# Attention and MoE kernel: which late weight parts a transfer adds, and where the second products stand at the two changes of block

## The chip, the cores and the metric

The kernel runs on one core of a Trainium2 chip. The metric is the device time of one execution in microseconds (us), median of several runs. Engines are named as the profile names them: PE (TensorE matmuls), PEld (its weight loads), DVE (VectorE), ACT (ScalarE), POOL (GpSimd), SP (SyncE, which here only issues DMAs).

## The reference

Linear attention feeds a two-layer MLP. All data are float32.

```python
q_s = softmax(q, over head_dim); k_s = softmax(k, over seq)   # 8 batches, 8 heads, 576 x 64
kv  = einsum('bhsd,bhse->bhde', k_s, v)
x   = einsum('bhsd,bhde->bhse', q_s, kv)      # reshaped to 4608 tokens x 512
h   = x @ w_in                                # 512 x 2048
out = (h * clip(h + 3, 0, 6) / 6) @ w_out     # 2048 x 512
```

The weights come as float64 and are turned into float32 on the chip.

## The kernel before

**Blocks and chunks.** The 4608 tokens are nine blocks j of 512. The 2048 hidden columns are 16 chunks f of 128; a chunk is one slice of w_in (512 x 128) and one of w_out (128 x 512). Every float32 operand of a product is kept as two parts, `hi` (rounded to float32r) and `lo` (what is left of it), and each product is three matmuls: hi by hi, hi by lo, lo by hi. `split` (L121) makes them: ACT casts hi, DVE subtracts lo.

**Weights.** `decode(f)` (L136) makes chunk f's parts. Its steps are ACT L148, DVE L149, L151 and L155, ACT L158, DVE L159 (the value `v` is complete), ACT L167 or L123 (hi). Then for f below 10 DVE subtracts lo; for f from 10 to 15 ACT writes lo = -v (L168) and a DMA from POOL's queue adds to it (L169). `hi` and `lo` there cover both halves of the chunk: `parts[:, 0]` is w_in's (`wi[f]`), `parts[:, 1]` is w_out's (`wo[f]`). The tile `v` has three buffers under one tag, and x's copies, the transposed q and `fast_weights`' sums take turns in the same three.

**Blocks 0 and 1.** `gemm1(j, f)` (L562) is the first product of a chunk: 12 matmuls `ph`, of which the third is the first one to read lo of w_in. ACT L572 and DVE L573 make g, `split` makes g_hi and g_lo. `gemm2` (L579) is the second product: 12 matmuls `po`, in block 0 from chunk 0 to 15, into four PSUM banks that stay open over all 16 chunks. The list `pend` holds second products that are not issued yet; `fill_one` (L674) issues the oldest whole, `fill(n)` (L665) issues n matmuls. In block 0 one second product stays back behind the newest; in block 1 none does (`1 - j`, L696). From block 1 on PE's instructions keep the order in which they are written (`in_order`, L684); in block 0 a scheduler orders them. `store` (L596) empties the four banks through the tile `ob` (two buffers), by turns on ACT and DVE.

**Attention** for the next block runs beside this as steps of a generator (`steps`, L636). A block's x comes out of `px` (four head pairs). For block 1, ACT and DVE cut px into x_hi and x_lo, and gemm1 of block 1 reads them. From block 2 on `x_factors` (L424) makes seven sums of x.

**Blocks 2 to 8** do the first products of a pair of chunks in seven products of half size (`fast_pair`, L498: `pz` and `ph`, 6 matmuls of 256 columns each) instead of eight. For that `fast_weights(pair)` (L451) makes sums of w_in's four quarters: two DVE adds L459 build the whole values, DVE L466, L467, L469 and L470 make four sums in two `ob` tiles, `split` writes their parts over the pair's own `wi` tiles, and SP stores them to DRAM (L456, L473). `fetch` (L486) loads the seven factors back into the tiles of chunks 6 to 11 as a ring. For pairs 0 to 6 `fast_weights` runs in block 1; for pair 7 it runs in the first pair of block 2, after the fourth `slot`. `slot(n)` (L703) issues n matmuls of the second products and, on its second and fourth call, one step of attention. Within `fast_pair`, ACT L524, L530, L534 and DVE L527, L535, L554 take the products out of PSUM; the results of a pair go into the tiles of chunks 12 to 15 (`places`, L520).

Of the kernel before, what the change touches and what calls it, by code (L numbers as in the profile page):

```python
# [10 lines left out]
F32 = mybir.dt.float32  # L11
# [3 lines left out]
ALU = mybir.AluOpType  # L15
# [15 lines left out]
def attention_moe(  # L31
# [27 lines left out]
    nc = tc.nc  # L59
# [5 lines left out]
    NFC = w.shape[0]  # L65
# [45 lines left out]
    def place(f, dt, name):  # L111
        return wp.tile([P, 4 * DM], dt, name=name, tag=f"w{f}")
# [6 lines left out]
    wi, wo, raws = {}, {}, {}  # L119

    def split(hi, lo, src, engine=nc.vector):  # L121

        nc.scalar.copy(hi, src)  # L123
        engine.tensor_sub(lo, src, hi.bitcast(F32))  # L124
# [9 lines left out]
    BY_DMA = 10  # L134

    def decode(f):  # L136

        n = 2 * DM
        pairs = raws.pop(f).rearrange("p (n two) -> p n two", two=2)
        low, high = pairs[:, :, 0], pairs[:, :, 1]
        v = moe.tile([P, n], F32, name="v", bufs=3)
        m = v
        nc.scalar.activation(m, high.bitcast(F32), AF.Abs)  # L148
        nc.vector.tensor_scalar(m, m, W_MIN, W_MAX, op0=ALU.max, op1=ALU.min)  # L149
        m = m.bitcast(U32)  # L150
        nc.vector.tensor_scalar(  # L151
            m, m, 3, 0x3FFFFFFF, op0=ALU.logical_shift_left, op1=ALU.bitwise_and
        )
        vu = v.bitcast(U32)
        nc.vector.scalar_tensor_tensor(  # L155
            vu, high, 0xC0000000, m, op0=ALU.bitwise_and, op1=ALU.bitwise_or
        )
        nc.scalar.activation(low, low, AF.Copy, scale=2.0**-29)  # L158
        nc.vector.tensor_tensor(vu, vu, low, op=ALU.add)  # L159
        parts = place(f, F32R, f"w_{f}").rearrange("p (s i n) -> p s i n", s=2, i=2)  # L160
        vs = v.rearrange("p (s n) -> p s n", s=2)
        if f < 10:
            split(parts[:, :, 0], parts[:, :, 1], vs)
        else:

            hi, lo = parts[:, :, 0], parts[:, :, 1]
            nc.scalar.copy(hi, vs)  # L167
            nc.scalar.mul(lo, vs, -1.0)  # L168
            nc.gpsimd.dma_start(lo.bitcast(F32), vs, accum_op=ALU.add)  # L169
        wi[f], wo[f] = parts[:, 0], parts[:, 1]  # L170

    FAST = 2
# [277 lines left out]

    def fast_weights(pair):  # L451

        a, b = wi[2 * pair], wi[2 * pair + 1]
        kept[pair] = d = dr.tile([P, 7, 2, HT], F32, name=f"wf{pair}")
        for n, src in ((A11, a[:, :, 0:HT]), (A12, a[:, :, HT:]), (A22, b[:, :, HT:])):
            nc.sync.dma_start(d[:, n], src.bitcast(F32))  # L456
        whole = moe.tile([P, 2 * DM], F32, name="m", tag="v", bufs=3)
        for at, src in ((0, a), (TB, b)):
            nc.vector.tensor_add(  # L459
                whole[:, at : at + TB], src[:, 0].bitcast(F32), src[:, 1].bitcast(F32)  # L460
            )
        a11, a12, a21, a22 = (whole[:, n * HT : (n + 1) * HT] for n in range(4))
        hi, lo = (t.rearrange("p e n -> p (e n)") for t in (a, b))
        s12, s34 = (moe.tile([P, DM], F32, name="ob", bufs=2) for _ in range(2))
        s1, s2, s3, s4 = (t[:, n : n + HT] for t in (s12, s34) for n in (0, HT))
        nc.vector.tensor_add(s1, a21, a22)  # L466
        nc.vector.tensor_sub(s2, s1, a11)  # L467
        split(hi[:, 0:TB], lo[:, 0:TB], s12)
        nc.vector.tensor_sub(s3, a11, a21)  # L469
        nc.vector.tensor_sub(s4, a12, s2)  # L470
        split(hi[:, TB:], lo[:, TB:], s34)
        for e, t in enumerate((hi, lo)):
            nc.sync.dma_start(  # L473
                d[:, S1 : S4 + 1, e], t.bitcast(F32).rearrange("p (k n) -> p k n", k=4)
            )
# [22 lines left out]
    def fast_pair(j, pair, fill):  # L498

        to = factors(j)  # L500
        x = ps_h.tile([P, TB], F32, name="ph", tag="ph")[:, 0:HT]
        y = ps_h.tile([P, TB], F32, name="ph", tag="ph")[:, 0:HT]
        z = ps_a.tile([P, TB], F32, name="pz", tag="pa")[:, 0:HT]
        seen = set()

        def product(n, ps, name):
            w_hi, w_lo = (come[j, pair, n][:, e] for e in (0, 1))
            f_hi, f_lo = (to[ORDER[n][1]][:, e] for e in (0, 1))
            for i in range(2):
                c = slice(i * P, (i + 1) * P)  # L510
                for k, (w, f) in enumerate(((w_hi, f_hi), (w_hi, f_lo), (w_lo, f_hi))):
                    first = name not in seen
                    seen.add(name)
                    mm(ps, w[:, c], f[:, i], first, i == 1 and k == 2, True)
            del come[j, pair, n]
            fetch(1)

        first = moe.tile([P, TB], F32, name="first", tag="g_hi", bufs=3)
        second = moe.tile([P, TB], F32, name="second", tag="g_lo", bufs=3)
        places = [wi[12 + 2 * (pair % 2) + n] for n in (0, 1)]  # L520
        product(0, z, "z")
        product(1, x, "x")
        with tc.high_priority():
            nc.scalar.copy(first[:, 0:HT], x)  # L524
        fill(4)
        product(2, y, "y")
        nc.vector.tensor_add(first[:, 0:HT], first[:, 0:HT], z)  # L527
        product(3, x, "x")
        with tc.high_priority():
            nc.scalar.copy(second[:, 0:HT], x)  # L530
        fill(7)
        product(4, x, "x")
        with tc.high_priority():
            nc.scalar.copy(second[:, HT:], x)  # L534
            nc.vector.tensor_add(second[:, HT:], second[:, HT:], y)  # L535
        fill(7)
        product(5, x, "x")
        r = moe.tile([P, TB], F32, name="g", bufs=2)
        with tc.high_priority():
            nc.scalar.activation(r[:, HT:], x, AF.Relu, bias=three, scale=1.0)  # L540
            nc.vector.scalar_tensor_tensor(  # L541
                r[:, HT:], r[:, HT:], 6.0, x, op0=ALU.min, op1=ALU.mult
            )
        h = first[:, 0:HT]
        nc.scalar.activation(r[:, 0:HT], h, AF.Relu, bias=three, scale=1.0)
        nc.vector.scalar_tensor_tensor(
            r[:, 0:HT], r[:, 0:HT], 6.0, h, op0=ALU.min, op1=ALU.mult
        )
        gs = [(places[0][:, 0], places[0][:, 1])]
        split(*gs[0], r)  # L550
        fill(6)
        product(6, y, "y")
        with tc.high_priority():
            nc.vector.tensor_add(second[:, 0:HT], second[:, 0:HT], y)  # L554
        r = moe.tile([P, TB], F32, name="g", bufs=2)
        nc.scalar.activation(r, second, AF.Relu, bias=three, scale=1.0)  # L556
        nc.vector.scalar_tensor_tensor(r, r, 6.0, second, op0=ALU.min, op1=ALU.mult)  # L557
        gs.append((places[1][:, 0], places[1][:, 1]))
        split(*gs[1], r)
        return gs  # L560
# [89 lines left out]
    pend = []  # L650
# [14 lines left out]
    def fill(n=10**6):  # L665
        while pend and n:
            got = next(pend[0], None)
            if got is None:
                pend.pop(0)
                continue  # L670
            got[0](*got[1])
            n -= 1

    def fill_one():  # L674
        for fn, x in pend.pop(0):
            fn(*x)

    for j in range(FAST):
        for f in range(NFC):
            if j == 0:  # L680
                if f + AHEAD < NFC:
                    load_w(f + AHEAD)
            elif not in_order:
                in_order.append(True)  # L684
            g = gemm1(j, f)
            if j == 0:
                if f + 2 < NFC:
                    decode(f + 2)
            elif f % 2:
                if f < 15:  # L690
                    fast_weights(f // 2)
                if f >= 7:
                    fetch(1 if f < 15 else 12 - len(come))
            next(step, None)

            while len(pend) > 1 - j:  # L696
                fill_one()
            pend.append(work(j, [f], [g]))
    for j in range(FAST, NB):
        for pair in range(NFC // 2):  # L700
            done = [0]

            def slot(n):  # L703
                fill(n)
                done[0] += 1
                if done[0] in (2, 4):
                    next(step, None)
                if j == FAST and not pair and done[0] == 4:
                    fast_weights(NFC // 2 - 1)

            gs = fast_pair(j, pair, slot)
            fill()
            pend.append(work(j, [2 * pair, 2 * pair + 1], gs))
# [60 lines left out]
```

## Time and profile before

| what | value |
|---|---|
| median of 3 runs | 892.21 us (889.02 to 894.39) |
| profiled execution, its own time | 890.79 us |
| its span, first to last instruction | 888.9 us |
| PE busy, share of the span | 858.4 us, 97% |
| DVE / ACT / POOL busy | 614.6 / 464.8 / 132.9 us |
| mean granted TensorE clock | 0.99 |
| block 0 ends, block 1 begins (PE) | about 144 us |
| block 1 ends, block 2 begins (PE) | about 244 us |

The time of an execution is 1.9 us more than its span. PE is the engine that ends the chain; what counts is therefore when PE waits, and at which clock it runs. In the timeline a row has the start in us, the busy time, the engine, the line, the operation with its tiles, and in brackets the idle time ahead of it and what ended that. In the windows a row has the stretch, its length, then the busy time of PE, PEld, DVE, ACT and POOL, the granted clock, the DMA share and GB/s. Most helpers record under one line (L91 is every matmul, L123 every cast of a split, L124 every subtraction of one), so tiles tell more than lines.

### The profile page before, as it was taken

Reading aid. Unit: us, or ns where it says so; the run is one execution under the profiler, and the core shown is the slowest. Engines: PE = TensorE matmul, PEld = TensorE weight load, DVE = VectorE, ACT = ScalarE, POOL = GpSimd, SP = SyncE. Lnnn points to the kernel's source line nnn. Section 1 sums busy time; section 2 is a strip of 40 time slices with the busy share of each in tenths; the row PEclk is TensorE's granted clock in tenths of the full one; section 3 lists DMA queues with packets and bytes.
Section 4 is the critical chain, followed back from the end, with each engine's and each line's share of the span. In section 5 each row is a group of like instructions: output and inputs, shape, how many; then the busy total and the mean of one; then the engine's idle time right before and its main releaser. Section 6 shows DMA issues by size and latency. Waiting matters only on the chain.

```text
span 888.9 us, 15262 instructions
## 1 busy us (share of the span) xinstructions
PE 858.4 (97%) x5380; PEld 739.2 (83%) x5380; DVE 614.6 (69%) x1266; ACT 464.8 (52%) x944; POOL 132.9 (15%) x329
## 2 busy tenths in 40 slices
PE   5799998999999999999999999999999999999998
PEld 3578776787789888888888888888888888889896
DVE  7999867899777766767585757676867565444333
ACT  7998753544445454545454545444554554434333
POOL 5000132021212110202020202021212120100000
PEclk9899999999999999999999999999999999999999
DMA  9992583538487668676777668676755575567541
GB/s 372 413 369 84 125 203 136 180 108 289 161 259 224 219 202 258 216 224 203 228 233 229 209 220 259 200 230 195 256 158 183 161 230 170 167 178 224 170 140 47
DMA packets 98474, 185.19 MB, mean 208 GB/s; under 512 B 9824, under 2 KB 24160, under 8 KB 96352
## 3 DMA queue, kind: packets, MB, share of 16 engines
q1 hardware_dynamic: 96192, 180.03, 62.3%
q0 software_dynamic: 1632, 3.15, 2.0%
q10 hardware_dynamic: 576, 1.05, 0.3%
q8 instruction: 43, 0.70, 0.3%
q14 instruction: 31, 0.25, 0.1%
HBM read 156.93 MB, written 24.12 MB: 204 GB/s over the span
## 4 chain that ended last, share of the span: by engine, by line
PE 83%; DVE 7%; DMA 6%; ACT 2%; issue 1%; POOL 0%; SPq 0%; ACTq 0%; DVEq 0%; POOLq 0%
PE po L91 41%; PE ph L91 33%; PE pz L91 4%; PE px L91 2%; PE pkv L91 2%; DMA w<-v 2%; DMA qt<-in_qf_dram 2%; DVE w L124 1%; DMA out_dram<-ob 1%; DVE v L155 1%; DVE v L149 0%; DMA wf<-w 0%; POOL swap L289 0%; DVE km L267 0%; DVE v L159 0%
## 5 line engine op out<-in xcount | busy, mean ns | idle before, releaser
L91 PE MATMUL po<-w,w 128*128 128x512 f32 x1008 | 260.8, 394 | 0.8 <-ACT w L123 0.8
L91 PEld LDWEIGHTS po<-w,w 128*128 128x128 f32 x1008 | 178.4, 189 | 30.7 <-ACT w L123 1.1
L91 PE MATMUL ph<-x_lo,w 128*128 128x256 f32 (+1 forms) x800 | 152.2, 305 | 2.7 <-DVE x_lo L124 2.3
L91 PEld LDWEIGHTS ph<-w,w 128*128 128x128 f32 x1008 | 133.8, 190 | 11.0 <-DVE second L535 1.4
L91 PE MATMUL ph<-x_hi,w 128*128 128x256 f32 (+1 forms) x592 | 138.4, 338 | 4.4 <-DMA w<-v 3.3
L91 PE MATMUL ph<-w,w 128*128 128x256 f32 x1008 | 140.4, 284 | 1.2 <-DVE second L535 1.2
L91 PEld LDWEIGHTS ph<-x_lo,w 128*128 128x128 f32 x800 | 117.0, 189 | 17.0 <-DVE x_lo L124 2.6
L91 PEld LDWEIGHTS ph<-x_hi,w 128*128 128x128 f32 x592 | 93.3, 191 | 18.8 <-DMA w<-v 3.5
L124 DVE TENSOR_TENSOR w<-g,w 128x512 fp32r<-128x512 f32 x112 | 77.2, 689 | 35.3 <-ACT w L123 35.3
L123 ACT CAST w<-g 128x512 fp32r<-128x512 f32 x112 | 69.4, 619 | 56.7 <-DVE g L541 34.4
L91 PE MATMUL po<-w 128*128 128x512 f32 x336 | 86.7, 394 | 0.1
L91 PEld LDWEIGHTS po<-w 128*128 128x128 f32 x336 | 59.4, 188 | 10.8 <-ACT w L123 0.5
L91 PE MATMUL po<-w,g_hi 128*128 128x512 f32 x256 | 67.4, 401 | 0.9 <-ACT g_hi L123 0.9
L556 ACT ACTIVATE g<-second,three 128x512 f32<-128x512 f32 x56 | 40.5, 724 | 33.9 <-DVE second L554 26.5
L91 PEld LDWEIGHTS po<-w,g_hi 128*128 128x128 f32 x256 | 47.7, 190 | 12.2 <-ACT g_hi L123 1.4
L540 ACT ACTIVATE g<-ph,three 128x256 f32<-128x256 f32 x56 | 26.6, 474 | 57.9 <-PE ph L91 57.9
L541 DVE SCALAR_TENSOR_TENSOR g<-g,ph 128x256 f32<-128x256 f32 x56 | 23.2, 415 | 47.1 <-ACT g L540 47.0
L534 ACT COPY second<-ph 128x256 f32<-128x256 f32 x56 | 20.8, 372 | 63.1 <-PE ph L91 63.1
L557 DVE SCALAR_TENSOR_TENSOR g<-g,second 128x512 f32<-128x512 f32 x56 | 39.0, 697 | 15.3 <-ACT g L556 15.2
L91 PE MATMUL pz<-x_hi,w 128*128 128x256 f32 x336 | 49.5, 283 | 0.0
L535 DVE TENSOR_TENSOR second<-second,ph 128x256 f32<-128x256 f32 x56 | 23.1, 413 | 37.5 <-ACT second L534 37.5
L289 POOL COPY swap<-qr 32x16 f32<-32x16 f32 x112 | 30.6, 273 | 96.4 <-DVE qr L301 92.8
(125 smaller groups left out, 1264.2 us busy)
## 6 DMA issues: line engine op xcount, KB each, us to landing
w<-wf SPq DMA_DIRECT2D x392, 256.0 KB, 3.0
raw<-in_w_dram SPq DMA_DIRECT2D x16, 1024.0 KB, 13.4
out_dram<-ob SPq DMA_DIRECT2D x36, 256.0 KB, 3.3
vt<-in_v_dram SPq DMA_DIRECT2D x28, 325.0 KB, 3.5
wf<-w SPq DMA_DIRECT2D x16, 512.0 KB, 4.7
kt<-in_kT_dram SPq DMA_DIRECT2D x28, 288.0 KB, 3.0
ke<-in_k_dram SPq DMA_DIRECT2D x24, 320.0 KB, 2.9
qt<-in_qf_dram SPq DMA_DIRECT2D x28, 256.0 KB, 3.0
```

The source lines that it names most:

```text
L91: nc.tensor.matmul(out, lhsT, rhs, start=start, stop=stop, skip_group_check=goes_on)
L123: nc.scalar.copy(hi, src)
L124: engine.tensor_sub(lo, src, hi.bitcast(F32))
L155: nc.vector.scalar_tensor_tensor(vu, high, 0xC0000000, m, op0=ALU.bitwise_and, op1=ALU.bitwise_or)
L289: nc.gpsimd.tensor_copy(swap[r : r + QD], stat[o : o + QD])
L534: nc.scalar.copy(second[:, HT:], x)
L535: nc.vector.tensor_add(second[:, HT:], second[:, HT:], y)
L540: nc.scalar.activation(r[:, HT:], x, AF.Relu, bias=three, scale=1.0)
L541: nc.vector.scalar_tensor_tensor(r[:, HT:], r[:, HT:], 6.0, x, op0=ALU.min, op1=ALU.mult)
L556: nc.scalar.activation(r, second, AF.Relu, bias=three, scale=1.0)
L557: nc.vector.scalar_tensor_tensor(r, r, 6.0, second, op0=ALU.min, op1=ALU.mult)
```

## The change

It does five things.

1. `decode`, f from 10 to 15: DVE now subtracts w_in's lo (L168 of the changed kernel, 128x512); only w_out's lo is written by ACT (L169) and added to by the DMA (L170), so both have half the size.
2. At the change from block 0 to 1 one second product (chunk 14) is issued ahead of the first gemm1 of block 1.
3. At the change from block 1 to 2 one second product more stays back: chunks 14 and 15 are both pending when block 2 begins, and four of their matmuls are issued ahead of the first product of its first pair.
4. `fast_weights(7)` runs with the others at the end of block 1, not inside block 2's first pair, so its SP transfers stand earlier too.
5. Its sums take the tiles of chunks 12 and 13 as scratch, which pair 6 has just used for its own.

```diff
 def decode(f):
-        if f < 10:
-            split(parts[:, :, 0], parts[:, :, 1], vs)
+        hi, lo = parts[:, :, 0], parts[:, :, 1]
+        nc.scalar.copy(hi, vs)
+        if f < BY_DMA:
+            nc.vector.tensor_sub(lo, vs, hi.bitcast(F32))
         else:
-            hi, lo = parts[:, :, 0], parts[:, :, 1]
-            nc.scalar.copy(hi, vs)
-            nc.scalar.mul(lo, vs, -1.0)
-            nc.gpsimd.dma_start(lo.bitcast(F32), vs, accum_op=ALU.add)
+            nc.vector.tensor_sub(lo[:, 0], vs[:, 0], hi[:, 0].bitcast(F32))
+            nc.scalar.mul(lo[:, 1], vs[:, 1], -1.0)
+            nc.gpsimd.dma_start(lo[:, 1].bitcast(F32), vs[:, 1], accum_op=ALU.add)
...
 def fast_weights(pair):
-        hi, lo = (t.rearrange("p e n -> p (e n)") for t in (a, b))
+        at = 2 * min(pair, NFC // 2 - 2)
+        hi, lo = (wi[at + n].rearrange("p e n -> p (e n)") for n in (0, 1))
...
 def fast_pair(j, pair, fill):
+        if (j, pair) == (FAST, 0):
+            fill(0)
         product(0, z, "z")
...
             elif not in_order:
                 in_order.append(True)
+                fill_one()
             g = gemm1(j, f)
...
             elif f % 2:
-                if f < 15:
-                    fast_weights(f // 2)
+                fast_weights(f // 2)
...
-            while len(pend) > 1 - j:
+            while len(pend) > (1 if j == 0 or f == NFC - 1 else 0):
                 fill_one()
...
             def slot(n):
-                fill(n)
+                fill(n or 4)
+                if not n:
+                    return
                 done[0] += 1
                 if done[0] in (2, 4):
                     next(step, None)
-                if j == FAST and not pair and done[0] == 4:
-                    fast_weights(NFC // 2 - 1)
```

The order on the engines is the same up to the decoding of chunk 10 and again from the third pair of block 2 on. It differs between, at these places.

**End of block 0, ACT.** In a name the number behind w_ is the chunk (w_13), then the buffer; v_950, v_1009, v_1061, v_1128 are the values of chunks 12 to 15 before, and v_952, v_1012, v_1065, v_1133 now. Before:

```order
L167 CAST w_12_957<-v_950 128x2x512
L168 ACTIVATE w_12_957<-v_950 128x2x512
L572 ACTIVATE g_1002<-ph_989,three_90 128x512
L268 ACTIVATE kt_1072<-kt_1072,km_1079 128x576
L364 COPY qT_916<-tp_911 128x512
L167 CAST w_13_1016<-v_1009 128x2x512
L168 ACTIVATE w_13_1016<-v_1009 128x2x512
L148 ACTIVATE v_1128<-raw15_869 128x1024
```

and now:

```order
L163 CAST w_12_959<-v_952 128x2x512
L169 ACTIVATE w_12_959<-v_952 128x512
L365 COPY qT_918<-tp_913 128x512
L269 ACTIVATE kt_1077<-kt_1077,km_1084 128x576
L123 CAST g_hi_1008<-g_1005 128x512
L148 ACTIVATE v_1133<-raw15_870 128x1024
L163 CAST w_13_1019<-v_1012 128x2x512
L169 ACTIVATE w_13_1019<-v_1012 128x512
```

The negated copy is 512 columns instead of 2 x 512, and chunk 15's first step, which needs the buffer of chunk 12's v, now stands ahead of chunk 13's cast instead of behind it.

**Change from block 0 to 1, PE.** w_305 is chunk 0's tile; w_1068 and w_1135 before, w_1072 and w_1140 now, are those of chunks 14 and 15; x_hi_539 and x_lo_540 are block 1's x. Before:

```order
L91 MATMUL ph<-x_hi_539,w_305 128x512 x2
L91 MATMUL ph<-x_lo_540,w_305 128x512
L91 MATMUL ph<-x_hi_539,w_305 128x512
L91 MATMUL px<-qT,kv 128x448
L91 MATMUL ph<-x_hi_539,w_305 128x512
L91 MATMUL ph<-x_lo_540,w_305 128x512
L91 MATMUL ph<-x_hi_539,w_305 128x512
L91 MATMUL po<-w_1068,g_hi 128x512 x8
L91 MATMUL po<-w_1068,g_lo 128x512 x4
L91 MATMUL po<-w_1135,g_hi 128x512 x2
```

and now:

```order
L91 MATMUL px<-qT,kv 128x64
L91 MATMUL po<-w_1072,g_hi 128x512 x8
L91 MATMUL po<-w_1072,g_lo 128x512 x4
L91 MATMUL ph<-x_hi_539,w_305 128x512
L91 MATMUL ph<-x_lo_540,w_305 128x512
L91 MATMUL ph<-x_hi_539,w_305 128x512 x2
L91 MATMUL ph<-x_lo_540,w_305 128x512
L91 MATMUL ph<-x_hi_539,w_305 128x512 x2
L91 MATMUL ph<-x_lo_540,w_305 128x512
L91 MATMUL ph<-x_hi_539,w_305 128x512
L91 MATMUL px<-qT,kv 128x448
L91 MATMUL ph<-x_hi_539,w_305 128x512
```

Chunk 14's twelve second products moved from behind the first gemm1 of block 1 to ahead of it; the last px still stands directly ahead of the matmuls that read what is made of it.

**Change from block 1 to 2, PE and DVE.** pz and ph with 256 columns are the first pair's products 0, 1, 2, 3. PE before:

```order
L91 MATMUL pkv<-vt,ke 64x65 x10
L91 MATMUL po<-w_1068,g_hi 128x512 x8
L91 MATMUL po<-w_1068,g_lo 128x512 x4
L91 MATMUL pz<-x_hi_310,w_588 128x256 x6
L91 MATMUL ph<-x_hi_310,w_588 128x256 x6
L91 MATMUL po<-w_1135,g_hi 128x512 x2
L91 MATMUL po<-w_1135,g_lo 128x512
L91 MATMUL po<-w_1135,g_hi 128x512
L91 MATMUL ph<-w_333,w_656 128x256 x6
L91 MATMUL ph<-w_305,w_656 128x256 x6
```

and now:

```order
L91 MATMUL pkv<-vt,ke 64x65 x10
L91 MATMUL po<-w_1072,g_hi 128x512 x4
L91 MATMUL pz<-x_hi_310,w_588 128x256 x6
L91 MATMUL ph<-x_hi_310,w_588 128x256 x6
L91 MATMUL po<-w_1072,g_hi 128x512 x4
L91 MATMUL ph<-w_333,w_656 128x256 x6
L91 MATMUL ph<-w_305,w_656 128x256 x6
L91 MATMUL po<-w_1072,g_lo 128x512 x4
L91 MATMUL po<-w_1140,g_hi 128x512 x2
L91 MATMUL po<-w_1140,g_lo 128x512
```

Eight of chunk 14's matmuls moved in between the products, and all of chunk 15's twelve stand behind product 3 (three stood ahead of product 2). On DVE the g here is chunk 13's, last in what stood before:

```order
L124 TENSOR_TENSOR x_hi_310<-v,x_hi_310 128x256
L124 TENSOR_TENSOR x_lo_311<-v,x_lo_311 128x256
L124 TENSOR_TENSOR w_305<-v,w_305 128x256
L124 TENSOR_TENSOR w_333<-v,w_333 128x256
L124 TENSOR_TENSOR w_365<-v,w_365 128x256
L290 TENSOR_TENSOR qm<-qm,swap 128x16
L124 TENSOR_TENSOR w_1016<-ob,w_957 128x512 x2
L299 TENSOR_TENSOR qt<-qt,qm 128x512
L573 SCALAR_TENSOR_TENSOR g<-g,ph 128x512
```

and now:

```order
L463 TENSOR_TENSOR m<-w_1072 128x512
L124 TENSOR_TENSOR x_hi_310<-v,x_hi_310 128x256
L463 TENSOR_TENSOR m<-w_1140 128x512
L124 TENSOR_TENSOR x_lo_311<-v,x_lo_311 128x256
L124 TENSOR_TENSOR w_305<-v,w_305 128x256
L124 TENSOR_TENSOR w_333<-v,w_333 128x256
L124 TENSOR_TENSOR w_365<-v,w_365 128x256
L291 TENSOR_TENSOR qm<-qm,swap 128x16
L124 TENSOR_TENSOR w_1019<-ob,w_959 128x512 x2
L580 SCALAR_TENSOR_TENSOR g<-g,ph 128x512
L300 TENSOR_TENSOR qt<-qt,qm 128x512
```

Pair 7's two adds now stand ahead of that g, and the subtraction on qt moved behind it.

## The prediction

> **What bounds the kernel now.** I read the page first, then the windows, PE's timeline where the windows show PE below its full time, and the chain of waits for PE's speed there. 0.5% (4.46 us) is about what a measurement of this kernel can tell from no change. The page's busy times:
>
> ```profile
> PE 858.4 (97%) x5380; PEld 739.2 (83%) x5380; DVE 614.6 (69%) x1266; ACT 464.8 (52%) x944; POOL 132.9 (15%) x329
> ```
>
> PE is the bound, so only its waits and its clock can be won. The windows show where it waits:
>
> ```profile
> 110.00:120.00 10.00, 7.04 (x24) 5.35 (x24) 6.60 (x13) 4.97 (x8) 3.12 (x6) 0.83 0.83 191
> 140.00:150.00 10.00, 7.05 (x29) 5.35 (x29) 8.01 (x18) 3.65 (x6) 2.93 (x11) 1.00 0.16 51
> 250.00:260.00 10.00, 8.32 (x50) 7.55 (x49) 7.83 (x19) 5.47 (x12) 1.77 (x5) 0.83 0.82 252
> 90.00:170.00 80.00, 73.80 (x366) 57.95 (x365) 61.58 (x116) 42.68 (x78) 14.18 (x31) 0.98 0.63 169
> 170.00:230.00 60.00, 60.00 (x313) 48.04 (x312) 53.37 (x114) 30.20 (x57) 15.48 (x37) 1.00 0.59 193
> ```
>
> Three stretches lose about 3 us each: the end of block 0, the change to block 1, the change to block 2. In two of them the granted clock is 0.83. PE's timeline names the waits (in brackets: us, and what ended them):
>
> ```profile
> 113.12 0.73 PE L91 MATMUL ph<-x_hi,w 128*128 128x512 f32 x2 [2.96 <-DMA w<-v]
> ...
> 133.66 0.73 PE L91 MATMUL ph<-x_hi,w 128*128 128x512 f32 x2 [0.30 <-DMA w<-v]
> ...
> 140.92 0.50 PE L91 MATMUL ph<-x_hi,w 128*128 128x512 f32 x1 [0.68 <-ACT x_hi L123]
> 143.69 0.51 PE L91 MATMUL ph<-x_lo,w 128*128 128x512 f32 x1 [2.27 <-DVE x_lo L124]
> ...
> 234.44 2.13 PE L91 MATMUL po<-w,g_hi 128*128 128x512 f32 x8 [0.54 <-ACT g_hi L123]
> ...
> 251.74 0.98 PE L91 MATMUL ph<-x_lo,w 128*128 128x256 f32 x6 [0.44 <-ACT second L534]
> 253.96 1.17 PE L91 MATMUL ph<-w,w 128*128 128x256 f32 x6 [1.24 <-DVE second L535]
> ```
>
> The first two are gemm1 of chunks 12 and 15 waiting for the adding transfer; the next two are gemm1 of block 1 waiting for its own last x; the last two are block 2's first pair waiting for its products to be taken out of PSUM. The chain of waits gives PE's speed behind two of them, and at full clock (start, us, what):
>
> ```profile
> 113.12 4.21 PE ph L91 x12
> 117.33 2.25 PE po L91 x8
> ...
> 150.00 2.79 PE ph L91 x12
> ...
> 152.90 2.78 PE po L91 x12
> ...
> 244.16 0.71 PE pz L91 x6
> ...
> 253.96 1.17 PE ph L91 x6
> 255.14 1.28 PE pz L91 x6
> 256.42 1.28 PE ph L91 x6
> 257.70 1.13 PE po L91 x4
> ```
>
> Behind the wait of 2.96 us, 20 matmuls took 6.46 us instead of 2.79 + 8/12 x 2.78 = 4.64: 1.81 us lost to the clock. Behind the wait of 1.24 us, 22 took 4.86 instead of 3 x 0.71 + 4/12 x 2.78 = 3.06: 1.80 us.
>
> **The late lower parts.** Rows of the tile v, ACT's and POOL's timeline, the DMA issues and the groups:
>
> ```profile
> L168 ACT ACTIVATE w<-v x6: 1056/1060/1066, 87.1 to 124.8; 128x1024 fp32r<-128x1024 f32 x6
> ...
> DMA to landing us min/median/max: 5.1/6.0/7.3
> ...
> 106.71 1.20 POOL L169 DMA_DIRECT2D w<-v  x1 [7.98 <-ACT w L168]
> ...
> 113.16 1.12 ACT L148 ACTIVATE v<-raw 128x1024 f32<-128x1024 f32 x1 [3.10 <-DMA w<-v]
> ...
> L124 DVE TENSOR_TENSOR w<-g,w 128x512 fp32r<-128x512 f32 x112 | 77.2, 689 | 35.3 <-ACT w L123 35.3
> ...
> wf<-w SPq DMA_DIRECT2D x16, 512.0 KB, 4.7
> wf<-w SPq DMA_DIRECT2D x24, 256.0 KB, 3.4
> ```
>
> Chunk 12's transfer, issued at 106.71, landed at 113.07 by the chain, and two things waited for it: gemm1, and chunk 15's first step on ACT (3.10 us), because it needs the buffer of chunk 12's v. Now gemm1 waits for a DVE subtraction of 0.69 us. Six of them are 4.1 us; DVE has 80 - 61.58 = 18.4 us idle between 90 and 170, so they lie beside PE's work, and are the price if that cover is gone. ACT gets less. The transfer still holds v, and ACT's order now puts chunk 15's first step ahead of chunk 13's cast, which so waits for chunk 12's landing and both (1.12 and about 0.9, 2.0 us). PE, without its wait, goes on at 113.12 - 2.96 = 110.16 and reads that cast 10 `ph` and 8 `po` later, at 114.35. The transfer of half the size takes between 3.4 us (plain, 256 KB) and 6.0 us (the whole, now); I take 4.7, a plain one's 512 KB row and also 6.0 less the 1.3 us between the plain rows. Landing at 111.4 the cast ends at 113.4, 0.9 us early. So both waits go, 3.26 us, and the dip behind the first, 1.81 us; bounds 0 and 5.07.
>
> By the Trainium skill (DMA: Bandwidth & Descriptors, "Anatomy of one DMA — SWDGE (gpsimd) path") such a transfer is about 2.0 us plus its bytes over 436 GB/s, so an estimate for half the size is 0.6 us less, not 1.3; the trace's 6.0 us for 512 KB is already twice what that fit gives, and the measurement decides. By it the cast would end at 114.1, still in time, and the sum stays.
>
> Second products of chunks 10 to 14 read w_out's lo at least one gemm1 (2.79 us) later than their first ones read w_in's; they wait for nothing I can see.
>
> **Change from block 0 to 1.** DVE and ACT there:
>
> ```profile
> 140.28 0.59 ACT L123 CAST x_hi<-px 128x512 fp32r<-128x512 f32 x1 [0.52 <-PE px L91]
> ...
> 142.13 0.17 DVE L290 TENSOR_TENSOR qm<-qm,swap 128x16 f32<-128x16 f32 x1 [0.47 <-POOL swap L289]
> ...
> 142.95 0.68 DVE L124 TENSOR_TENSOR x_lo<-px,x_hi 128x512 fp32r<-128x512 f32 x1
> ```
>
> The last x_lo could have begun at 140.9, when x_hi was there, and began at 142.95, behind a softmax that waited for POOL. Chunk 14's second products give DVE 2.78 us more before px comes, and in the new order on DVE that POOL wait stands behind x_lo. From the last `pkv`, PE's road to px is about 8.2 us (10 `ph`, 16 `po`, 9 `ph` and small ones); x_hi comes some 1.4 us later (px about 0.8, then 140.24, where PE began to wait, to the cast's end at 140.87), at 9.6. DVE has 18 operations before x_lo, 13 of them of 0.6 to 0.7 us, about 9 us together. So x_lo begins as soon as x_hi is there. No PE work that needs neither stands behind px, so 0.68 stays, and of 2.27 what is left is 2.27 - 2.05 = 0.22: 0.90 of 2.95 stays, 2.05 goes. Bounds: 0 (each us that DVE is late beyond 0.6 stays) and 2.05. As chunk 15's products now end sooner after chunk 14's, block 0's store has less time for its two `ob` tiles before block 1 needs the banks: I charge 0.3 (bounds 0 and 1.0).
>
> **Change from block 1 to 2.**
>
> ```profile
> 228.29 0.69 DVE L297 TENSOR_REDUCE qm<-qt 128x16 f32<-128x512 f32 x1 [2.90 <-DMA qt<-in_qf_dram]
> ...
> 233.06 0.67 DVE L573 SCALAR_TENSOR_TENSOR g<-g,ph 128x512 f32<-128x512 f32 x1
> ...
> 233.77 0.62 ACT L123 CAST g_hi<-g 128x512 fp32r<-128x512 f32 x1
> ...
> 249.69 1.25 DVE L459 TENSOR_TENSOR m<-w 128x512 f32<-128x512 f32 x2
> ...
> 252.56 0.69 DVE L604 TENSOR_SCALAR ob<-po 128x512 f32<-128x512 f32 x1 [1.62 <-DMA out_dram<-ob]
> 253.17 0.41 DVE L124 TENSOR_TENSOR x_hi<-v,x_hi 128x256 fp32r<-128x256 f32 x1
> 253.50 0.41 DVE L535 TENSOR_TENSOR second<-second,ph 128x256 f32<-128x256 f32 x1
> ```
>
> The add at 253.50, for which PE waited, stood behind pair 7's adds (1.25) and a store that waited 1.62 for an `ob` tile. The first go to block 1; and with 24 matmuls to put in between, PE has 7 to 8 of them (1.6 to 1.9 us) behind each product whose result must leave PSUM. So 0.44 + 1.24 = 1.68 goes, and the dip of 1.80; bounds 0 and 3.48. Against that, pair 7's two adds (1.25) stand ahead of chunk 13's g, which PE already waits for (0.54), and one operation of 0.6 no longer does; the DMA wait of 2.90 ahead of them doesn't shrink. I charge 0.5 (bounds 0 and 1.3). Pair 7's sums reuse the tiles that pair 6's transfers still read, so ACT and DVE wait for those to land; the matmuls behind are g of chunks 14 and 15, whose products now stand 2 to 5 us later: nothing. Of the SP queue, pair 7's two stores stand ahead of block 3's key and value loads and the ring's next loads; those ring loads need product 0 first (after 244.16), and DVE's last of the sums is done before: nothing.
>
> **The sum.** 3.26 + 1.81 + 2.05 - 0.3 + 1.68 + 1.80 - 0.5 = 9.8 us. The profiled execution took 890.79 (span 888.9 and 1.9 around it), 1.42 below the median of the runs, and becomes 881.0; from the median, 892.21, the time is **882.4**. With the two charges at nothing it is 881.6, and the fastest run shown lies 3.19 below its median, so this case begins at 879.0; it ends at 886, with 3.6 us of the unsure terms not won.
>
> **The rivals.**
>
> *The clock stays as it is.* Both dips follow a wait here, but the wait of 0.68 + 2.27 us at 140 to 144 was followed by none (1.00 in that window). If the dips fall where they fall for another reason, 3.61 us stay: -6.2, 886.0. The Trainium skill (TensorE: Matmul & The Clock Gate, "Why this matters for your kernels") says that only idle gaps of over about 3 us bring the clock down; by it neither 2.96 nor 1.68 us would. The trace has a dip behind each. Chance 0.10.
>
> *The adding transfer holds PE by way of ACT.* At 7.3 us, as the longest now, chunk 12's lands at 114.0, chunk 13's cast ends at 116.0, PE waits 1.65 us and loses 1.81 to a dip: -6.3, 885.9. ACT's 3.10 wait speaks for it, the halved size against. Chance 0.08.
>
> *DVE keeps its pace.* It is busy 53.37 of 60 us from 170 to 230. If it can't start block 1's sums sooner, what PE wins by 144 it waits for again by 230, and only the change to block 2 is won: -3.0, 889.2. Against it: the timeline has no PE wait between 144 and 234, and DVE waits for PE's releases there. Chance 0.14.
>
> *Slower: VectorE becomes the bound.* It needs 61.58 + 4.1 = 65.7 us between 90 and 170, and PE's road there would be 80 - 7.1 = 72.9. If more than 7.2 of its 18.4 idle us are waits that stay, PE waits for it; if all stay, nothing is won and the subtractions (4.1) and pair 7's adds (1.25) come on top: +5.3, 897.5. But 5 us of that idle were waits for the adding transfer. Chance 0.06.
>
> **Numbers.** Forecast 0.62, and it is the likeliest: 882.4. It and the first two rivals are faster by over 0.5% (below 887.75): 0.80. Within 0.5%: 0.14. Slower: 0.06. The range runs from 879.0 to 889.5, which leaves out the slower case and the forecast's ends.
>
> **What would show it.** Right: no PE wait on w<-v near 113 and 133; the last x_lo wait before block 1's second gemm1 under 0.5 us; no wait on second L542 in block 2's first pair; a wait on chunk 13's g_hi near 1 us; clock 1.00 in the windows of these places. Wrong: a wait on chunk 13's cast, PE waits on g_lo or g_hi inside block 1, or a dip of the clock in a new place (each 1.8 us).

## The result and the profile after

The changed kernel takes **882.55 us** (median of 6 runs, 882.21 to 883.86) against 892.12 for the kernel before (6 runs on the same chip): a ratio of 0.9897, 95% interval 0.988 to 0.9914. The profiled execution took 882.21, 8.58 less than the one of before; its span is 880.4, 8.5 less. The prediction said 882.4, and 9.8 less for the profiled execution. So the median was met, but between the two traces 1.2 us are missing; where they went is the most useful part below.

The page's busy times of the changed kernel:

```profile
PE 852.5 (97%) x5380; PEld 734.2 (83%) x5380; DVE 616.4 (70%) x1272; ACT 462.7 (53%) x944; POOL 131.8 (15%) x329
```

DVE has its six subtractions more, but its busy time rose by 1.8 us and not by their 4.1; other instructions took 2.3 less, which I did not trace. The windows of the changed kernel, in the columns of those of before:

```profile
110.00:120.00 10.00, 10.00 (x45) 8.10 (x44) 8.18 (x14) 5.47 (x8) 1.27 (x3) 1.00 0.61 167
220.00:230.00 10.00, 8.20 (x35) 6.04 (x35) 7.37 (x17) 2.25 (x5) 2.22 (x5) 1.00 0.34 114
240.00:250.00 10.00, 9.65 (x64) 8.64 (x63) 6.54 (x14) 5.51 (x13) 1.50 (x5) 1.00 0.86 290
```

The window with chunk 12 is full and at full clock, and no window behind 40 us is below 1.00 any more (two at the start, from 20 to 40, are at 0.89 and 0.77; before, they were at 0.84 and 0.69). New is the hole from 220 to 230, in a stretch where PE was full before. PE's timeline names what is left:

```profile
138.70 0.49 PE L91 MATMUL ph<-x_hi,w 128*128 128x512 f32 x1 [0.68 <-ACT x_hi L123]
139.43 0.50 PE L91 MATMUL ph<-x_lo,w 128*128 128x512 f32 x1 [0.23 <-DVE x_lo L124]
215.60 0.44 PE L91 MATMUL px<-qT_hi,kv_lo 128*128 128x384 f32 x1 [0.52 <-DVE kv_lo L124]
223.97 1.20 PE L91 MATMUL po<-w,g_lo 128*128 128x512 f32 x4 [0.49 <-DVE g_lo L124]
229.38 2.13 PE L91 MATMUL po<-w,g_hi 128*128 128x512 f32 x8 [1.31 <-ACT g_hi L123]
248.69 0.99 PE L91 MATMUL ph<-x_hi,w 128*128 128x256 f32 x6 [0.35 <-DVE g L548]
```

No wait on the adding transfer; 0.91 us at the change to block 1; three waits late in block 1, of which only the one of 1.31 was there before (0.54); and one small one in block 2's second pair. The chain of waits gives the same places to set beside those of before:

```profile
142.93 2.80 PE ph L91 x12
...
229.38 3.04 PE po L91 x12
...
249.68 0.93 PE po L91 x4
```

Block 1's second first product, 150.00 before, now starts at 142.93: 7.07 us won. Chunk 13's second product, 234.44 before, starts at 229.38: 5.06 are left. The first `po` in block 2's second pair, 257.70 before, starts at 249.68: 8.02.

### The profile page after: what moved, and what is told of

Read it like the earlier page. It is cut to its first block, busy times and chain, and to the rows that moved or that the text cites. A ratio compares the mean times of both kernels' runs of the same rounds, so it can differ in the third digit from the quotient of the medians.

```text
span 880.4 us, 15263 instructions
## 1 busy us (share of the span) xinstructions
PE 852.5 (97%) x5380; PEld 734.2 (83%) x5380; DVE 616.4 (70%) x1272; ACT 462.7 (53%) x944; POOL 131.8 (15%) x329
## 4 chain that ended last, share of the span: by engine, by line
PE 87%; DVE 7%; ACT 2%; DMA 2%; issue 1%; POOL 0%; ACTq 0%; DVEq 0%; POOLq 0%
PE po L91 42%; PE ph L91 34%; PE pz L91 4%; PE px L91 3%; PE pkv L91 3%; DMA qt<-in_qf_dram 1%; DVE v L155 1%; DMA out_dram<-ob 1%; DVE w L165 1%; DVE v L149 0%; DVE w L124 0%; DVE x_lo L124 0%; DMA kq<-in_kT_dram 0%; DVE v L159 0%; DVE v L151 0%
## 5 line engine op out<-in xcount | busy, mean ns | idle before, releaser
L91 PE MATMUL ph<-x_hi,w 128*128 128x256 f32 (+1 forms) x592 | 136.5, 334 | 1.3 <-ACT x_hi L123 0.7
```

What stands on the lines that cost most here:

```text
L91: nc.tensor.matmul(out, lhsT, rhs, start=start, stop=stop, skip_group_check=goes_on)
```

## The experiments

The theory (A in the expectations): three places lose time independently, two of them with a dip of the clock behind the wait, and the gains add up. The rivals: the dips fall wherever they fall (B); VectorE keeps its pace, and PE waits later for what it won earlier (C); the parts hold pieces of each other's gain (K). Each ratio below is to the kernel before, run on the same chip in the same set; a gain in us is one minus the ratio, times 892.

### Each part alone

The decode part alone, the first of the three, is the first hunk of the change put into the kernel before:

```diff
...
-            nc.scalar.mul(lo, vs, -1.0)
-            nc.gpsimd.dma_start(lo.bitcast(F32), vs, accum_op=ALU.add)
+            nc.vector.tensor_sub(lo[:, 0], vs[:, 0], hi[:, 0].bitcast(F32))
+            nc.scalar.mul(lo[:, 1], vs[:, 1], -1.0)
+            nc.gpsimd.dma_start(lo[:, 1].bitcast(F32), vs[:, 1], accum_op=ALU.add)
```

> The kernel before with the decode part of the change alone. Theory A (three independent places whose gains add up): the waits on w<-v at 113 and 133 are gone and so is the dip of the clock behind the first, 3.26 + 1.81 = 5.1 us, so about 887.0; the waits at the change to block 1 (0.68 and 2.27) and the dip near 250 stay. Rival B (the clock falls there whatever waits): the window of 110 to 120 stays at 0.83 and only 3.3 us are won, 888.8. Rival C (VectorE keeps its pace): the last x_lo of block 1 comes no sooner, PE waits there for what it won, and the time stays within 1.5 us of before.

Measured: 885.86 against 893.71, ratio 0.9926 (0.9898 to 0.9953): 6.6 us won (4.2 to 9.1). Its windows and PE's waits:

```profile
110.00:120.00 10.00, 10.00 (x45) 8.11 (x44) 8.10 (x14) 5.01 (x7) 1.70 (x4) 1.00 0.66 174
240.00:250.00 10.00, 8.72 (x59) 7.70 (x59) 6.27 (x13) 4.92 (x11) 0.85 (x1) 1.00 0.80 242
250.00:260.00 10.00, 10.00 (x73) 8.47 (x71) 8.91 (x20) 6.12 (x13) 1.47 (x5) 1.00 0.95 298
```

```profile
137.84 0.50 PE L91 MATMUL ph<-x_lo,w 128*128 128x512 f32 x1 [0.95 <-DVE x_lo L124]
...
246.61 0.98 PE L91 MATMUL ph<-x_lo,w 128*128 128x256 f32 x6 [0.44 <-ACT second L535]
248.43 0.98 PE L91 MATMUL ph<-w,w 128*128 128x256 f32 x6 [0.84 <-DVE second L536]
```

Both waits and the dip at 114 are gone, as A has it. But x_lo also comes 1.3 us less late (0.95 for 2.27), though nothing was changed there, and the waits in block 2's first pair stand with no dip behind them.

The second: only the second product of chunk 14 ahead of block 1.

```diff
                 in_order.append(True)
+                fill_one()
```

> The kernel before with the second product of chunk 14 ahead of block 1's first product, and nothing else. Theory A: of the waits of 0.68 + 2.27 us about 0.9 stays and a charge of 0.3 comes on, -1.75 us, about 890.4; the waits of 2.96 at 113 and of 0.44 + 1.24 in block 2's first pair stay, each with its dip of 1.8 us. Rival C (VectorE keeps its pace, and PE waits later for what it won): within 0.5 us of before.

Measured: 890.77 against 893.71, ratio 0.9974 (0.9957 to 0.9991): 2.3 us (0.8 to 3.8). Its window with chunk 12, and its waits:

```profile
110.00:120.00 10.00, 6.97 (x24) 5.39 (x24) 6.31 (x11) 4.79 (x8) 2.88 (x5) 0.83 0.87 204
```

```profile
113.42 0.73 PE L91 MATMUL ph<-x_hi,w 128*128 128x512 f32 x2 [3.03 <-DMA w<-v]
...
250.92 0.98 PE L91 MATMUL ph<-x_lo,w 128*128 128x256 f32 x6 [0.44 <-ACT second L534]
252.81 0.98 PE L91 MATMUL ph<-w,w 128*128 128x256 f32 x6 [0.91 <-DVE second L535]
```

The wait at 113 keeps its dip. The pair's waits of 0.44 and 0.91 again have none: the six matmuls take 0.98, and the clock is 1.00 in all windows from 240 to 270.

The third: second products kept back, and pair 7's sums in block 1, with the first two parts undone.

```diff
-                if f < 15:
-                    fast_weights(f // 2)
+                fast_weights(f // 2)
...
-            while len(pend) > 1 - j:
+            while len(pend) > (1 if j == 0 or f == NFC - 1 else 0):
...
```

> The kernel before with the three parts at the change from block 1 to 2 alone. Theory A: 1.68 us of waits and the dip of 1.80 behind them go, 0.5 comes on at chunk 13's g, -3.0, about 889.1; the first two places stay as they were, with the dip at 113. Rival B (the dip near 250 has another cause): the dip stays and -1.2 is left, 890.9. If A holds for all three, the three gains of this set add up to the 9.6 us of the whole change.

Measured: 891.32 against 893.71, ratio 0.9978 (0.9962 to 0.9994): 2.0 us (0.5 to 3.4). The waits on the second tile are gone; the one on chunk 13's g_hi, 0.54 before, is 1.34 us, though PE comes there no earlier than before (the `pkv` at the start of block 1 is at 158.99, before at 158.40):

```profile
235.73 2.12 PE L91 MATMUL po<-w,g_hi 128*128 128x512 f32 x8 [1.34 <-ACT g_hi L123]
```

At 113 it waits 3.21 us, and the window of 110 to 120 is at 0.83.

Together the three win 10.9 us by these ratios, the whole change 9.2 to 9.9 (two sets); by the plain medians it is 13.2 against 9.6 and 10.0. So A holds as a sum only within wide intervals. Part by part the 5.1 and 3.0 us that it gives for the first and the third lie inside their intervals too, but the waits show that the decode part is worth more than its own waits, and the last one less. Rival B falls at 113 (the dip goes with the wait, and stays in both kernels that keep it), and is left open at 250.

The first two parts together, without the third:

> The kernel before with the decode part and the change from block 0 to 1, without the three parts at the change from block 1 to 2. Theory A (the places add up): the third place is still to be won, so 2.0 to 3.0 us slower than the changed kernel. Theory K (the gain of the decode part alone, 7.9 us, already holds part of the later ones, because VectorE comes sooner everywhere behind it): within 1 us of the changed kernel, or about as fast as the decode part alone.

Measured: 885.67 against 892.88, ratio 0.992 (0.9892 to 0.9949), 2.8 us slower than the changed kernel in the same set, though the intervals overlap. In its profile the third place costs less than at home (0.44 and 0.87 us, no dip), and the loss has moved to the change from block 2 to 3:

```profile
345.15 1.20 PE L91 MATMUL po<-w,w 128*128 128x512 f32 x4 [2.41 <-ACT w L123]
```

```profile
340.00:350.00 10.00, 7.59 (x41) 6.83 (x40) 6.34 (x13) 3.91 (x8) 0.76 (x4) 0.83 0.80 246
```

The chain leads that wait through ScalarE to a store of block 2 that took 4.99 us to land; in the changed kernel the same one took 3.43, and PE waits 0.85. So neither A nor K is quite right, as far as one profile can say: the 2.8 us are A's size, at another place in this one execution.

### The third place taken apart

Pair 7's sums back inside block 2's first pair, the rest of the change as it is:

> The changed kernel with pair 7's sums back inside block 2's first pair; the second products are still kept back. Theory A: the matmuls between the products cover those sums, no wait on a product of the first pair comes back, and the wait of 1.31 us on chunk 13's g_hi falls to about 0.5, so 0.5 to 0.8 us faster than the changed kernel, about 881.9. Rival D (moving the sums is what freed the pair): the wait on the second tile comes back with 0.5 to 1.7 us, and with the clock's dip of 1.8 behind it, 884.5 to 885.5.

Measured: 885.71 against 893.71, ratio 0.9918 (0.9895 to 0.9941); by the ratios 1.9 to 2.6 us slower than the changed kernel (two sets), though the intervals overlap. Its waits in block 1 and block 2:

```profile
228.54 2.13 PE L91 MATMUL po<-w,g_hi 128*128 128x512 f32 x8 [0.73 <-ACT g_hi L123]
...
248.16 0.99 PE L91 MATMUL ph<-x_hi,w 128*128 128x256 f32 x6 [0.67 <-DVE g L547]
...
272.31 0.98 PE L91 MATMUL ph<-w,w 128*128 128x256 f32 x6 [0.91 <-DVE second L541]
```

At 229 it wins 0.6, as A said, and it is 0.53 ahead at 248. Then PE waits in block 2's second and third pairs (0.67, between these rows 0.40 and 0.22, then 0.91): 1.85 more than the changed kernel, whose only wait there is the 0.35. The span ends 3.5 us later; the rest of that has no one place. The kept products alone don't cover the sums: rival D, with the waits one and two pairs later than I had them, and without a dip.

The other half undone: sums early, nothing kept back.

```diff
-        if (j, pair) == (FAST, 0):
-            fill(0)
...
-            while len(pend) > (1 if j == 0 or f == NFC - 1 else 0):
+            while len(pend) > 1 - j:
```

> The changed kernel with the sums of pair 7 in block 1, but second products no longer kept back at the change from block 1 to 2. The run with those sums late lost about 3 us. Theory F (the place of the sums is what counts there): no more than 0.5 us slower than the changed kernel, 882.5 to 883. Theory G (the kept products count as well): waits of 0.4 to 1.3 us on the second tile in the first pair of block 2, 883.5 to 884, and 885.5 if the clock dips behind them.

Measured: 884.9 against 893.33, ratio 0.9906 (0.9886 to 0.9926), and PE's waits in block 2's first pair:

```profile
246.94 0.98 PE L91 MATMUL ph<-x_lo,w 128*128 128x256 f32 x6 [0.70 <-ACT second L541]
249.53 0.98 PE L91 MATMUL ph<-w,w 128*128 128x256 f32 x6 [1.60 <-DVE second L542]
```

The waits of 2.3 us are theory G's, and larger than it had them. By the ratios it is 0.8 to 1.5 us slower than the changed kernel, inside the intervals, so here the waits say more than the time. By the waits both halves are needed; neither alone frees block 2's first three pairs.

### Does the transfer still earn its place?

```diff
-    BY_DMA = 10
+    BY_DMA = NFC
```

> The changed kernel with no adding transfer: VectorE subtracts both lower parts of chunks 10 to 15 too, some 0.6 us more for each of six chunks, 3.6 us. Theory A (VectorE has room near the end of block 0, the transfer's wait was the cost): within 1 us of the changed kernel, 882 to 883.5, with no new wait of PE between 100 and 140. Rival E (VectorE is at its limit there, the transfer still earns its place): PE waits for VectorE between 100 and 145 and 2 to 3.6 us are lost, 884.5 to 886.

Measured: 883.98 against 893.33, ratio 0.9907 (0.9884 to 0.993), which can't be told from the changed kernel. In its profile PE waits at one place near the end of block 0:

```profile
141.51 0.50 PE L91 MATMUL ph<-x_hi,w 128*128 128x512 f32 x1 [1.96 <-ACT x_hi L123]
142.36 0.50 PE L91 MATMUL ph<-x_lo,w 128*128 128x512 f32 x1 [0.34 <-DVE x_lo L124]
```

That is 2.30 instead of 0.91, so some 1.4 us are lost there. The wait is on ScalarE's x_hi, and ScalarE's timeline shows that cast behind a step of the attention that waited for VectorE:

```profile
140.36 0.63 ACT L301 ACTIVATE qt<-qt 128x512 f32<-128x512 f32 x1 [0.93 <-DVE qt L300]
140.89 0.57 ACT L123 CAST x_hi<-px 128x512 fp32r<-128x512 f32 x1
```

So VectorE reaches PE here by way of ScalarE, as rival E has it in the wait, if not in the size; the scheduler also put the second products at the end of block 0 in other places, so not all of it need be the subtractions'. With some 3.6 us more work VectorE takes 1.4 us of PE's time at the end of block 0 in this execution and nothing that the runs can tell: the rival with 897.5 was far off.

### What gave back time late in block 1

VectorE's timeline of the changed kernel shows two waits of the next attention unit ahead of PE's new waits (they were 0.81 and 2.90 before):

```profile
207.64 0.69 DVE L298 TENSOR_REDUCE qm<-qt 128x16 f32<-128x512 f32 x1 [1.32 <-DMA qt<-in_qf_dram]
...
222.63 0.69 DVE L298 TENSOR_REDUCE qm<-qt 128x16 f32<-128x512 f32 x1 [3.39 <-DMA qt<-in_qf_dram]
```

The chain has the two loads with their issue and the time to their landing, in the kernel before:

```profile
207.01 7.17 DMA qt<-in_qf_dram
...
224.32 3.94 DMA qt<-in_qf_dram
```

and in the changed kernel:

```profile
200.34 7.28 DMA qt<-in_qf_dram
...
218.02 4.58 DMA qt<-in_qf_dram
```

They were issued 6.67 and 6.30 us earlier than before and landed 6.56 and 5.66 earlier, where PE had won 7.07. Everything queued on VectorE behind the reduction waits with it: at 222.63 chunk 12's g_lo, pair 7's two adds, chunk 13's g. To test that, four adds (of pairs 6 and 7) go to GpSimd:

```diff
-            nc.vector.tensor_add(
+            (nc.gpsimd if pair > 5 else nc.vector).tensor_add(
```

> The changed kernel with the two adds of pairs 6 and 7 (four of 0.64 to 0.68 us) on GpSimd instead of VectorE; PE's order is the same. Theory H (VectorE, late in block 1, gave back some 2 us of what was won): the waits of 0.49 on g_lo near 224 and of 1.31 on g_hi near 229 fall to 0.5 or less together, 0.8 to 1.5 us faster than the changed kernel, about 881.4. Rival I (VectorE there only waits for the load of qt, 3.39 us, whatever it has to do): the same waits, the same time, 882.5. Slower than the changed kernel if GpSimd is so slow that its sums hold the weights of pair 7.

Measured: 882.27 against 893.33, ratio 0.9879 (0.9861 to 0.9897). In the profile PE has no wait at all from 140 to 246, and is 2.3 us ahead of the changed kernel there (246.38 for 248.69); 1.1 us of it is left at the end of the span. It was run once more, beside the changed kernel:

> The kernel with the adds of pairs 6 and 7 on GpSimd, once more beside the changed kernel. Theory H: its waits in block 1 are gone, 1.0 to 2.0 us faster than the changed kernel of this set; rival: the same, because a wait at the next change of block (340) grows by what was won.

> The changed kernel once more, beside the three others of this set. Expected: 0.988 to 0.991 of before; it is the mark for the others, since single medians of one kernel differed by 1 to 2 us between sets.

Measured: 882.52, ratio 0.9879 (0.9856 to 0.9903), and 882.89, ratio 0.9889 (0.9868 to 0.9911), for the changed kernel: the same, by the measurement. The second profile says why. VectorE's reduction in the first, and in the second:

```profile
206.01 0.69 DVE L298 TENSOR_REDUCE qm<-qt 128x16 f32<-128x512 f32 x1
```

```profile
208.78 0.69 DVE L298 TENSOR_REDUCE qm<-qt 128x16 f32<-128x512 f32 x1 [2.95 <-DMA qt<-in_qf_dram]
...
216.14 0.34 DVE L219 SCALAR_TENSOR_TENSOR kv<-pkv,rk,mask 128x128 f32<-128x128 f32 x1
```

and PE's timeline of the second:

```profile
216.87 0.44 PE L91 MATMUL px<-qT_hi,kv_hi 128*128 128x384 f32 x1 [2.06 <-ACT kv_hi L123]
...
217.77 3.21 PE L91 MATMUL po<-w,g_hi 128*128 128x512 f32 x8
```

One and the same kernel: in the first execution the load was there in time, in the second it took 8.04 us to land (by the chain), kv came out late behind it, PE waited 2.06 us, and the next eight matmuls took 3.21 instead of 2.13. So between these two executions the landing of this load decides when block 1 ends. Theory H is right about the waits of the first, but less work on VectorE buys nothing that can be measured while the load's landing differs by more than it. The direct test, a load of qt that is issued earlier, was not made.

All sixteen adds on GpSimd:

> The changed kernel with these adds of all eight pairs on GpSimd, sixteen of 0.64 us off VectorE. With the adds of two pairs moved PE has no wait left between 140 and 240, so theory H expects the same time as there, within 0.5 us. Rival: GpSimd's own time for them comes ahead of its small copies for the softmax, VectorE waits for these, and 1 us or more is lost.

Measured: 885.5 against 892.88, ratio 0.9923 (0.9899 to 0.9947): 2.6 us slower than the changed kernel in its set. The rival was right on the size and wrong on the way. VectorE, GpSimd and PE in its profile:

```profile
223.93 3.29 DVE L124 TENSOR_TENSOR w<-v,w 128x256 fp32r<-128x256 f32 x3
224.14 2.79 POOL L463 TENSOR_TENSOR m<-w 128x512 f32<-128x512 f32 x2
230.40 2.12 PE L91 MATMUL po<-w,g_hi 128*128 128x512 f32 x8 [2.42 <-ACT g_hi L123]
```

Three subtractions, which take 1.08 together in the changed kernel, took 3.29 while GpSimd's two adds ran; chunk 13's g stands behind them on VectorE, and PE's wait on its g_hi grew to 2.42. Two more waits of PE, 0.88 at 189 and 0.80 at 197, are not there in the changed kernel.

### Waits made on purpose

Between blocks 3 and 8 the changed kernel has long stretches without a wait of PE. There ScalarE copied a product out of PSUM several times over, so that PE, which needs the bank, waited as long as the copies took (pair 5 likewise, for two products):

```diff
         with tc.high_priority():
-            nc.scalar.copy(first[:, 0:HT], x)
+            for _ in range(1 + 2 * (j - 1) * (j > FAST and pair == 2)):
+                nc.scalar.copy(first[:, 0:HT], x)
```

> The changed kernel with made waits of PE in a stretch that has none: in blocks 3 to 8 ScalarE copies a product out of PSUM 5, 7, 9, 11, 13 and 15 times instead of once (pair 2), and two products running 5 to 10 times each (pair 5). Theory J (the granted clock falls behind a wait of PE when the wait is long enough): waits under about 1.5 us leave the clock at 1.00, waits of about 3 us bring 0.83 in their window of 10 us, and the border shows between. Rival B (dips come at their own places): the clock stays at 1.00 behind all of them. The output is the same; the time, some 10 to 30 us more, says nothing.

PE's timeline: the wait, and then the busy time of the next six matmuls, 0.97 to 0.99 at full clock. (The one execution took 942.02 us; its length is made by the waits and says nothing.)

```profile
399.19 0.97 PE L91 MATMUL ph<-x_lo,w 128*128 128x256 f32 x6 [1.75 <-ACT second L544]
...
494.11 1.27 PE L91 MATMUL ph<-x_lo,w 128*128 128x256 f32 x6 [2.69 <-ACT second L539]
...
554.22 0.98 PE L91 MATMUL ph<-w,w 128*128 128x256 f32 x6 [2.45 <-ACT first L532]
595.07 1.65 PE L91 MATMUL ph<-x_lo,w 128*128 128x256 f32 x6 [3.60 <-ACT second L539]
...
762.11 1.65 PE L91 MATMUL ph<-w,w 128*128 128x256 f32 x6 [5.65 <-ACT first L532]
801.65 1.54 PE L91 MATMUL ph<-x_lo,w 128*128 128x256 f32 x6 [2.08 <-ACT second L539]
...
900.60 1.51 PE L91 MATMUL ph<-x_lo,w 128*128 128x256 f32 x6 [2.49 <-ACT second L539]
```

Theory J, with a border that is no line: up to 1.75 us no made wait brought the clock down, 2.08, 2.49 and 2.69 did, 2.45 did not, and 3.27 (its windows are at 0.92 and 0.91), 3.60, 3.71, 4.87 and 5.65 all did.

## Why the prediction came out as it did

**The late lower parts: right.** 3.26 us of waits and the dip of 1.81 were to go, and did, alone and with the rest. The half-size transfer lands in 3.3, 4.0 and 6.0 us (least, median, longest of six) where I took 4.7 between 3.4 and 6.0. ScalarE's timeline of the changed kernel shows chunk 15's first step and, behind it, chunk 13's cast:

```profile
110.41 1.13 ACT L148 ACTIVATE v<-raw 128x1024 f32<-128x1024 f32 x1 [2.16 <-DMA w<-v]
111.44 1.04 ACT L163 CAST w<-v 128x1024 fp32r<-128x1024 f32 x1
```

The wait for chunk 12's transfer is still there, as foreseen, and ends at 110.41 where I had 111.4; the cast ends at 112.48 where I had 113.4. The rival by way of ScalarE did not come.

**Change from block 0 to 1: right in size.** 0.90 was to stay, and 0.91 did. The charge of 0.3 for the store does not show: by 142.93 PE has won 7.07, and without the charge the terms up to there are 7.12. What I had not seen is that most of this gain needs no kept product: the decode part alone brings x_lo's wait from 2.27 to 0.95, so behind it the second part is worth some 0.7 us, not 1.75. The terms were of the right sum and wrongly given to their edits.

**The step that failed** is the one that left the stretch between the two changes out of the sum. Of 7.07 us, 5.06 are left at 229. I weighed "DVE keeps its pace" as a rival that takes everything or nothing, and in the sum charged 0.5 for the adds ahead of chunk 13's g. The runs show a part of it: 0.77 at that g, and 0.52 + 0.49 at two new waits, 1.78 of the 2.01. They are two different losses.

Of the 0.77, some 0.6 is the price of the adds, near the 0.5 that was charged: VectorE's way from the start of its reduction to that g takes 4.77 us before (228.29 to 233.06) and 5.38 in the changed kernel (222.63 to 228.01). It comes with the place of the adds and not with PE's gain: the wait on that g_hi is 1.34 with the third part alone, where PE comes no earlier, 0.73 with the sums late and the rest of the change kept, and 0.58 with the first two parts.

The rest and the two new waits stand behind VectorE's waits for the loads of qt, one of which is the 2.90 us in the row I quoted. The sum took it that this wait "doesn't shrink" and charged nothing for it; it grew to 3.39. A load does come earlier when the work that issues it does, only not always by the whole gain: 6.56 and 5.66 of 7.07 here. With the first two parts alone PE has won 6.0 us early in block 1, and VectorE's two reductions, at 214.20 and 228.29 before, start 5.87 and 5.84 earlier:

```profile
208.33 0.69 DVE L298 TENSOR_REDUCE qm<-qt 128x16 f32<-128x512 f32 x1 [0.94 <-DMA qt<-in_qf_dram]
...
222.45 0.69 DVE L298 TENSOR_REDUCE qm<-qt 128x16 f32<-128x512 f32 x1 [2.39 <-DMA qt<-in_qf_dram]
```

There 5.83 us are left at chunk 13's second product, so nearly nothing is lost. How much of a gain passes these loads differs from execution to execution: in the second profile of the changed kernel the new wait on g_lo is 0.66, the one on kv_lo is not there, and the one on g_hi is 1.31 again. The wait on g_lo inside block 1 is one of the signs of being wrong that the prediction had named.

**Change from block 1 to 2: the waits right, the dip not.** Of 0.44 + 1.24 only a new 0.35 is left. But the 1.80 of the dip was taken from one execution. With waits of 0.44 and 0.84, of 0.44 and 0.91, and even of 0.70 and 1.60, the clock stays at 1.00 there in the profiles of the runs above. So it is no steady part of the price, and the part alone wins 2.0 us and not 3.0, though 3.0 lies inside its interval (0.5 to 3.4). From 229 to 250 the change wins 8.02 - 5.06 = 3.0 us between the two profiled executions, against 3.48 in the sum.

**The total.** Between the two profiles the misses are 1.0 (the two new waits), 0.3 (chunk 13's g), 0.35 (the new wait in block 2), less 0.3 (the charge not needed): about 1.3, where 1.2 were missing. The median came out at the forecast for another reason too: the profiled execution of before lay 1.42 below the median it was set against and that of the changed kernel 0.34 below its own, so the medians differ by more than the profiles. The median was hit partly by that, which is luck. (The lower end of the range doesn't follow from its own terms: 881.6 less 3.19 is 878.4, not 879.0.)

## What to carry to other kernels

When PE gains time, follow the gain through the loads that the next waits stand behind: compare the issue and the landing of each before and after, since a load that comes earlier by less than PE does is a new wait. Price work that is moved ahead of a result PE waits for separately from that gain. Price a clock dip behind a wait of 2 to 3 us as a chance and not as a certainty, and look at more than one execution. A part's worth depends on what stands ahead of it, so a set of edits is measured each alone and all together before one of them is given the credit.

## What the hardware showed that I had not expected

- **The clock's border is wide.** Behind 100 us in all profiles here, single waits of 2.06, 2.08, 2.41, 2.49 and 2.69 us had a dip behind them (a window of 10 us below 1.00); 2.42 and 2.45 had none, nor had 2.27 and 2.33 with 0.68 shortly ahead. From 2.96 up all eight had one. Of single waits up to 1.96 none had; the only smaller case is the pair of 0.44 and 1.24 before. The Trainium skill (TensorE: Matmul & The Clock Gate, "What's actually happening") says that activity is watched in a window of about 3.4 us that runs freely; a wait would then count by how it lies in that window, which agrees with a border that depends on more than the length. That waits of only 2.1 us can do it is not in its rule of about 3 us, and the measurement decides.
- **GpSimd can hold VectorE up.** Three subtractions of 1.08 us took 3.29 beside two GpSimd adds, while the adds took 2.79 and, beside a waiting VectorE, 2.55. The Trainium skill (SBUF — State Buffer, "SBUF: two separate sides") says that a GpSimd operation and a VectorE operation with two inputs in SBUF take turns at a shared pair of ports, one whole instruction at a time. The trace agrees, and also shows the way out: in the kernel with four adds moved, the last two ran while VectorE waited 3.29 us for its load, and cost it nothing; the first two stretched one subtraction from 0.41 to 1.01 us.
- **An adding transfer is slow by its size, too.** 256 KB landed in 4.0 us (median) and 512 KB in 6.0, so, as an estimate from these two sizes alone, 2.0 us for each 256 KB. The longest of the smaller ones also took 6.0.
